# Segmented attention with memory beside a Fourier mixing: the order inside an attention piece, the lead of the row loads, the layout of the stored values

## The chip, the cores and the metric

The kernel runs on one core of one Trainium2 chip, as one launch. The metric is the time on the device in microseconds (us), lower is better. Engines are named as in the profile: PE (matmuls), DVE (VectorE), ACT (ScalarE), POOL (GpSimd), and SP (SyncE), whose queue SPq issues every DMA of this kernel.

## The reference

Two independent parts share the launch, and their outputs stand side by side in the last axis. B is 1, S is 2048, D is 576.

```
# part A: H = 32 heads of Dh = 18, N = 4 segments of L = 512
q, k, v = heads(x @ wq), heads(x @ wk), heads(x @ wv)
for s in range(N):
    logits = qs @ ks^T * Dh**-0.5 + mask   # mask: -1e9 where the key is later than the query
    a_dot  = softmax(logits) @ vs
    pq     = phi(qs)                       # phi(t) = t + 1 for t > 0, else exp(t)
    a_mem  = (pq @ M) / (pq @ z + 1e-6)
    o      = g * a_mem + (1 - g) * a_dot   # g = sigmoid(beta), one per head
    M += phi(ks)^T @ vs ;  z += sum(phi(ks))
A = concat(o) @ wo
# part B
B = dft_seq_re @ (x @ dft_hid_re^T) - dft_seq_im @ (x @ dft_hid_im^T)
out = concat([A, B], axis=-1)
```

## The kernel before, in words

Products in float32 are made from parts: a rounded high part and the remainder, three matmuls for each product. Queries and keys are cut into three bf16 parts, and six pairs of parts (6 x 18 = 108 rows, `NPAIR`) are stacked on the contraction axis, so that one matmul makes scores.

**Projection (first 235 us).** Four segments, one after the other. `project_qk(s, m)` makes nine blocks of queries and keys (m = 0 to 3 queries, 4 to 7 keys, 8 the rest of both); its inner `rest` makes the second and third part and sends them to DRAM (`qd`, `kd`). `project_v(s, j)` makes values for 128 rows and sends them, in three parts with a column of ones, to `vd`: 55 columns a head, 220 for a group of four heads. `load_wv` loads the weights of the values; each is split three ticks later by `split_wk`.

**Attention (235 to about 990 us).** Heads are taken in 32 groups G of four (eight groups in each segment). A loop over pieces p handles two heads in each: `attention()` yields eight times in a piece, after slots 0 to 7, whose weights are `SLOTS`. After each yield the driver runs `tick()`, which calls everything that `later(n, ...)` put off to this tick, and then as much of `dense()` (part B) as the weight stands for. So the order on every engine is fixed when the program is built: the order of the calls is the order of each engine's queue, and no engine overtakes in its own queue. What belongs to heads 2p and 2p + 1 is spread over later pieces by `F_LAG` = 2, `T_LAG` = 3 and `V_LAG` = 4.

- The first head of a piece ("even"): `s_fill` makes scores and DVE takes their row maxima; `t_fill` makes the scores again, transposed, three pieces later; ACT takes the exponential, and `pv` multiplies with the values four pieces after `s_fill`. `t_fill` reads 111 rows of `qs`: the 108 and three more that hold the row maxima.
- The second head ("odd"): `f_fill` makes scores and maxima, `f_exp` the exponential, `f_split_hi` and `f_split_lo` two fp16 parts `hl` (ACT, DVE, POOL), and `f_turn` turns them with a DMA transpose on SP into `ptt`, which `pv` reads.
- `stack_load(G)` loads twelve blocks of 72 KB, six to `qs` and six to `ks`, four in each of the next three ticks, and after `lag` ticks the values `vst`. There are three buffers of `qs` and `ks` (`G % 3`). `s_fill` of group G starts with slot 0 of piece 2G; the last reader of the same buffer is `t_fill` kind 2 of group G - 3, in slot 4 of piece 2G - 2.
- `maxima(p // 2)` runs in slot 4 of every odd piece, when both even heads of the group have their maxima. `maxima_transpose` turns them on PE a few ticks later, copies them on ACT to `mt`, sends them to DRAM (`md`) with a DMA in the next tick, and some ticks later a second DMA brings them as three rows into `qs` (`qs<-md`). The first `t_fill` of group G, in slot 1 of piece 2G + 3, needs these three rows.

PSUM has three banks for part B (`d`), two for scores (`s`), two for transposed scores (`t`), one for `pv`.

**Output (last 65 us).** Part A's heads are joined, transposed and multiplied by `wo`.

Of the kernel before, what the change touches and what calls it, by code (L numbers as in the profile page):

```python
# [15 lines left out]
BF16 = mybir.dt.bfloat16  # L16
AF = mybir.ActivationFunctionType
# [5 lines left out]
S, D, H, DH, NSEG, L = 2048, 576, 32, 18, 4, 512  # L23
P = 128
# [5 lines left out]
NPAIR = 108  # L30
# [6 lines left out]
def infini_attention_and_fnet(ctx: ExitStack, tc: tile.TileContext, xT, wqk, w8, wv, wo, beta, xtT, cT, hT, out):  # L37
    nc = tc.nc
    act, dve, pool, pe = nc.scalar, nc.vector, nc.gpsimd, nc.tensor
    dma = nc.sync.dma_start  # L40
    ctx.enter_context(tc.manual_schedule())
    const = ctx.enter_context(tc.tile_pool(name="const", bufs=1))
    dram = ctx.enter_context(tc.tile_pool(name="dram", bufs=1, space=DRAM))
# [1 line left out]

    qd = [dram.tile([D, 3, L], BF16, name=f"qd{s}") for s in range(NSEG)]
    kd = [dram.tile([D, 3, L], BF16, name=f"kd{s}") for s in range(NSEG)]
    vd = [dram.tile([P, 4, 8, 220], BF16, name=f"vd{s}") for s in range(NSEG)]
    amd = [dram.tile([P, D], F32, name=f"amd{t}") for t in range(NT)]
    md = [dram.tile([24, P], BF16, name=f"md{g}") for g in range(32)]  # L50
    yd = [dram.tile([P, D], F32, name=f"yd{t}") for t in range(NT)]
# [2 lines left out]
    def split(hi, lo, raw, lo_engine=None):  # L54
        act.activation(hi, raw, AF.Copy)  # L55
        (lo_engine or dve).tensor_tensor(lo, raw, hi.bitcast(F32), OP.subtract)  # L56
# [10 lines left out]
    g = const.tile([P, H], F32, name="g")  # L67
# [8 lines left out]
    def chain(o, terms):  # L76
        for n, (a, b) in enumerate(terms):
            pe.matmul(o, a, b, start=n == 0, stop=n == len(terms) - 1)  # L78
# [3 lines left out]
    def later(n, fn, *a):  # L82
        due.setdefault(clock[0] + n, []).append((fn, a))
# [84 lines left out]
        later(3, split_wk, WV, k, load_w(wv, D, k))  # L168

    for k in range(5):  # L170
        later(3 + k, load_wv, k)
    later(5, gates)

    pq_hi = sb.tile([P, 5, L], F32R, name="pq_hi")
# [6 lines left out]
    for i in range(2):  # L181
# [5 lines left out]
        t = sb.tile([P, H, 55], BF16, name=f"vs{i}")  # L187
# [13 lines left out]
    def qk_terms(s, m):  # L201
        xh, xl, xt = X[s]
        W, c = (WQ, m) if m < 4 else (WK, m - 4) if m < 8 else (W8, 0)
        cs = slice(c * P, (c + 1) * P)
        terms = []
        for k in range(4):
            terms += [(W[0][k][:, cs], xh[k]), (W[0][k][:, cs], xl[k]), (W[1][k][:, cs], xh[k])]
        return terms + [(W[2][:, cs], xt), (W[3][:, cs], xt)]
# [20 lines left out]
    def project_qk(s, m):  # L229
        if m in FIRST:  # L230
            o = FIRST.pop(m)
        else:
            o = ps.tile([P, L], F32, name="qk", tag="acc", bufs=4)
            chain(o, qk_terms(s, m))
        if m >= 4 and s < 3:
            KF[m] = sk.tile([P, L], F32, name="kf", bufs=5)
            act.activation(KF[m], o, AF.Copy)
        p = sb.tile([P, 3, L], BF16, name="p", bufs=4)
        r = sb.tile([P, L], F32, name="r", bufs=2)
        act.activation(p[:, 0], o, AF.Copy)  # L240
        dve.tensor_tensor(r, o, p[:, 0], OP.subtract)  # L241
        if s and (m < 4 or m == 8):
            n = P if m < 4 else 64
            c = m if m < 4 else 4
            phi(sb, "q", o[:n], n, pq_hi[:n, c], pq_lo[:n, c])

        def rest():
            act.activation(p[:, 1], r, AF.Copy)
            pool.tensor_tensor(p[:, 2], r, p[:, 1], OP.subtract)
            if m < 8:  # L250
                later(1, dma, (qd if m < 4 else kd)[s][(m % 4) * P:(m % 4 + 1) * P], p)
            else:
                later(1, dma, qd[s][4 * P:], p[:64])
                later(1, dma, kd[s][4 * P:], p[64:])

        later(1, rest)
# [9 lines left out]
    def project_v(s, j, meanwhile):  # L266
        xh, xl, xt = X[s]
        js = slice(j * P, (j + 1) * P)
        vs = vs_bufs[j % 2]
        r = sb.tile([P, H, DH], F32, name="vr", bufs=2)  # L270
        for h in range(2):
            cs, hs = slice(h * 288, (h + 1) * 288), slice(16 * h, 16 * h + 16)
            o = ps.tile([P, 288], F32, name="v", tag="acc", bufs=4)
            terms = []
            for k in range(4):
                terms += [(xh[k][:, js], WV[1][k][:, cs]), (xh[k][:, js], WV[0][k][:, cs]),
                          (xl[k][:, js], WV[0][k][:, cs])]
            terms += [(xt[:, js], WV[2][:, cs]), (xt[:, js], WV[3][:, cs])]
            chain(o, terms)
            o = o.rearrange("p (h d) -> p h d", d=DH)  # L280
            act.activation(vs[:, hs, 18:36], o, AF.Copy)
            if s < 3:
                split(vn[j % 2][0][:, hs, :DH], vn[j % 2][1][:, hs, :DH], o)
            dve.tensor_tensor(r[:, hs], o, vs[:, hs, 18:36], OP.subtract)
            next(meanwhile, None)
        if s < 3 and j == 3:
            for k in range(2, 5):
                split_x(s + 1, k)

        act.activation(vs[:, :, 36:54], r, AF.Copy)  # L290
        pool.tensor_tensor(vs[:, :, 0:18], r, vs[:, :, 36:54], OP.subtract)
        later(1, dma, vd[s][:, j], vs.rearrange("p (g h) c -> p g (h c)", g=8))

    started = set()

# [88 lines left out]
    qs_bufs, ks_bufs, VS = [], [], {}  # L384
# [18 lines left out]

    NG = 32

    def stack_load(G, lag=23):
        if G >= NG:
            return
        s, g8 = divmod(G, 8)
        rows = slice(g8 * 72, g8 * 72 + 72)  # L410
        for buf, src, parts in ((qs_bufs[G % 3], qd[s], QPARTS), (ks_bufs[G % 3], kd[s], KPARTS)):
            for c, part in enumerate(parts):
                later(1 + c // 2, dma, buf[18 * c:18 * c + 18],
                      src[rows, part, :].rearrange("(h d) t -> d h t", d=DH))

        def values():
            VS[G] = sa.tile([P, 4, 220], BF16, name="vst", bufs=3)
            dma(VS[G], vd[s][:, :, g8])
        later(lag, values)

    for s in range(NSEG):
# [277 lines left out]
    def maxima(G):  # L699
        m, b = NEGM[G % 2], MB[G % 2][:, :24].rearrange("p (c n) -> p c n", c=3)  # L700
        r = sa.tile([P, 8], F32, name="negx", bufs=2)
        pool.tensor_copy(b[:, 0], m)
        pool.tensor_tensor(r, m, b[:, 0], OP.subtract)
        pool.tensor_copy(b[:, 1], r)
        pool.tensor_tensor(b[:, 2], r, b[:, 1], OP.subtract)
        later(5, maxima_transpose, G)

    def maxima_transpose(G):
        t = ps.tile([P, P], BF16, name="trm", tag="t")
        pe.transpose(t, MB[G % 2], ident16)  # L710
        w = sa.tile([24, P], BF16, name="mt", bufs=2)
        act.activation(w, t[:24], AF.Copy)
        later(1, dma, md[G], w)
        later(5, dma, qs_bufs[G % 3][NPAIR:NPAIR + 3, 0:4:2], md[G].rearrange("(c h n) t -> c h (n t)", c=3, h=2))

    def t_fill(n, kind):
        G, h = divmod(n, 4)
# [71 lines left out]
    F_LAG, T_LAG, V_LAG = 2, 3, 4  # L789
# [3 lines left out]
    def attention():  # L793
        for p in range(NP + V_LAG):
            def even(lag, fn, *a):
                if 0 <= p - lag < NP:
                    fn(2 * (p - lag), *a)

            def odd(lag, fn, *a):
                if 0 <= p - lag < NP:  # L800
                    fn(2 * (p - lag) + 1, *a)

            if p == 2:
                stacks(sa, 2)
            if p == NP + 1:
                o_load(0)
                o_load(1)
            if p % 2:
                stack_load(p // 2 + 1)
            even(0, s_fill, 0)  # L810
            odd(F_LAG + 1, f_exp, 2)
            odd(F_LAG + 1, f_split_hi)
            yield SLOTS[0]
            even(T_LAG, t_fill, 0)
            odd(F_LAG + 1, f_split_lo)
            yield SLOTS[1]
            even(0, s_fill, 1)
            even(T_LAG, t_fill, 1)
            yield SLOTS[2]
            even(0, s_fill, 2)  # L820
            even(V_LAG, pv)
            even(T_LAG, t_lo, 1)
            yield SLOTS[3]
            odd(F_LAG, f_fill, 0)
            even(T_LAG, t_fill, 2)
            if p % 2 and p < NP:
                maxima(p // 2)
            yield SLOTS[4]
            odd(F_LAG, f_fill, 1)
            odd(V_LAG, pv)  # L830
            even(T_LAG, t_hi)
            even(T_LAG, t_lo, 2)
            yield SLOTS[5]
            odd(F_LAG, f_exp, 0)
            if p >= V_LAG:
                pv_out(p - V_LAG)
            yield SLOTS[6]
            odd(F_LAG, f_exp, 1)
            odd(F_LAG, f_fill, 2)
            even(T_LAG, t_lo, 0)  # L840
            odd(F_LAG + 1, f_turn)
            yield SLOTS[7]
# [7 lines left out]
    for w in attention():  # L850
        tick()
        ta += w
        while td / total_d < ta / total_a:
            t = next(d, BREAK)
# [65 lines left out]
```

## Time and profile before

| what | value |
|---|---|
| time, median of 3 runs | 1069.86 us (1066.59 to 1076.57) |
| the profiled execution: its own time, its span | 1068.58 us, 1066.9 us |
| mean granted clock of PE | 0.99 |
| busy share of the span: PE, DVE, ACT, POOL | 97%, 72%, 65%, 57% |
| PE busy from 242 us to 1000 us | 733.0 of 758.0 us |
| DMA queue q1: packets, bytes, share of the 16 DMA engines | 287616, 192.81 MB, 74.5% |
| row loads `qs<-qd` and `ks<-kd` | 384 DMAs of 72 KB |
| `vd<-vs`, `vst<-vd` | 16 DMAs of 440 KB, 32 of 220 KB |
| DMA transposes `ptt<-hl` | 64 |

A group of instructions is told by line, engine, operation and tile, with its busy time, the mean duration of one, and the idle time of its engine just before it with what ended that idle time. Matmuls are pipelined, so their durations overlap; what one costs is the distance from its start to the next one's. "PEclk" is the granted share of PE's clock. SPq's rows are issues: their duration is how long the issue held SP's queue, not how long the data took.

### The profile page before, as it was taken

Reading aid. Unit: us, or ns where it says so; the run is one execution under the profiler, and the core shown is the slowest. Engines: PE = TensorE matmul, PEld = TensorE weight load, DVE = VectorE, ACT = ScalarE, POOL = GpSimd, SP = SyncE. Lnnn points to the kernel's source line nnn. Section 1 sums busy time; section 2 is a strip of 40 time slices with the busy share of each in tenths; the row PEclk is TensorE's granted clock in tenths of the full one; section 3 lists DMA queues with packets and bytes.
Section 4 is the critical chain, followed back from the end, with each engine's and each line's share of the span. In section 5 each row is a group of like instructions: output and inputs, shape, how many; then the busy total and the mean of one; then the engine's idle time right before and its main releaser. Section 6 shows DMA issues by size and latency. Waiting matters only on the chain.

```text
span 1066.9 us, 25805 instructions
## 1 busy us (share of the span) xinstructions
PE 1031.3 (97%) x9464; PEld 952.7 (89%) x9464; DVE 764.1 (72%) x2095; ACT 695.3 (65%) x1474; POOL 602.8 (57%) x655
## 2 busy tenths in 40 slices
PE   9999999999999999999999999999899998999998
PEld 8888989889998999888988899999898898889998
DVE  6545647574887787678888888889778788776343
ACT  6667575654876777676776777776666676666233
POOL 2456565755765667556666676666565566557000
PEclk9999999999999999999999999999999999999999
DMA  7525253366668888798988999799898999878474
GB/s 237 179 81 182 85 182 136 123 232 181 148 158 196 195 181 198 172 200 216 203 194 191 206 187 177 167 207 198 206 207 187 219 206 192 218 175 182 139 203 142
DMA packets 287742, 194.45 MB, mean 182 GB/s; under 512 B 210496, under 2 KB 242816, under 8 KB 287616
## 3 DMA queue, kind: packets, MB, share of 16 engines
q1 hardware_dynamic: 287616, 192.81, 74.5%
q8 instruction: 74, 1.21, 0.5%
q14 instruction: 52, 0.43, 0.1%
HBM read 106.84 MB, written 43.97 MB: 141 GB/s over the span
## 4 chain that ended last, share of the span: by engine, by line
PE 78%; ACT 7%; DVE 6%; DMA 4%; issue 3%; POOL 2%; SPq 0%; DVEq 0%; POOLq 0%; ACTq 0%
PE d L480 33%; PE s L651 6%; PE d L78 6%; PE v L78 4%; PE d L526 3%; PE pv L768 3%; PE d L527 3%; PE d L528 3%; PE qk L225 2%; DMA craw<-cT 2%; PE pv L769 2%; PE qk L78 1%; DVE r L241 1%; PE look L329 1%; PE t L727 1%
## 5 line engine op out<-in xcount | busy, mean ns | idle before, releaser
L657 DVE CUSTOM_DVE_ANT_0 s<-s,causal 128x512 f32<-128x512 f32 (+3 forms) x512 | 252.9, 496 | 76.3 <-PE s L651 68.5
L56 POOL TENSOR_TENSOR clo<-craw,chi 128x512 fp32r<-128x512 f32 x158 | 217.9, 1380 | 153.6 <-ACT chi L55 122.1
L480 PE MATMUL d<-wide,chi 128*128 128x288 f32 x1408 | 266.1, 306 | 0.0
L480 PEld LDWEIGHTS d<-wide,chi 128*128 128x128 f32 x1408 | 212.2, 191 | 4.6 <-issue 3.7
L480 PE MATMUL d<-wide,clo 128*128 128x288 f32 x704 | 175.9, 317 | 0.0
L680 ACT ACTIVATE pf<-s,nb 128x512 f32<-128x512 f32 (+3 forms) x256 | 127.6, 528 | 57.6 <-DVE nb L672 56.9
L651 PE MATMUL s<-ks,qs 108*128 108x512 bf16 (+3 forms) x512 | 136.1, 307 | 23.8 <-DMA craw<-cT 6.5
L737 ACT ACTIVATE phi<-t 128x384 f16<-128x384 f32 x128 | 62.5, 488 | 102.9 <-PE t L734 83.7
L751 DVE TENSOR_TENSOR plo<-pf,phi 128x384 f16<-128x384 f32 (+1 forms) x128 | 125.6, 981 | 2.3 <-ACT pf L738 2.3
L480 PE MATMUL d<-ab,chi 128*128 128x288 f32 x640 | 126.2, 307 | 0.0
L480 PEld LDWEIGHTS d<-wide,clo 128*128 128x128 f32 x704 | 117.4, 192 | 1.5
L692 POOL TENSOR_TENSOR hl<-pf,hl 128x768 f16<-128x768 f32 x64 | 108.5, 1696 | 0.0
L55 ACT ACTIVATE chi<-craw 128x512 fp32r<-128x512 f32 x160 | 100.6, 629 | 11.6 <-PE d L480 11.5
L738 ACT ACTIVATE pf<-t 128x384 f32<-128x384 f32 (+1 forms) x192 | 99.5, 518 | 11.1 <-PE t L727 10.9
L741 POOL TENSOR_SCALAR_AFFINE_SELECT pf<-pf 128x512 f32<-128x512 f32 x64 | 44.9, 701 | 102.0 <-ACT pf L738 97.4
L480 PEld LDWEIGHTS d<-ab,chi 128*128 128x128 f32 x640 | 99.0, 192 | 0.8
L687 ACT ACTIVATE hl<-pf 128x768 f16<-128x768 f32 (+1 forms) x128 | 87.4, 729 | 2.0
L480 PE MATMUL d<-ab,clo 128*128 128x288 f32 x320 | 84.7, 314 | 0.0
L526 PE MATMUL d<-wide,chi 128*128 128x288 f32 x256 | 82.9, 324 | 0.0
L651 PEld LDWEIGHTS <-qs 108*128 108x128 bf16 x512 | 40.0, 98 | 46.1 <-issue 13.7
L527 PE MATMUL d<-wide,chi 128*128 128x288 f32 x256 | 75.6, 295 | 0.0
L528 PE MATMUL d<-wide,clo 128*128 128x288 f32 x256 | 75.5, 295 | 0.0
(197 smaller groups left out, 2543.0 us busy)
## 6 DMA issues: line engine op xcount, KB each, us to landing
craw<-cT SPq DMA_DIRECT2D x128, 256.0 KB
qs<-qd SPq DMA_DIRECT2D x192, 72.0 KB
ks<-kd SPq DMA_DIRECT2D x192, 72.0 KB
craw<-xtT SPq DMA_DIRECT2D x32, 320.0 KB
out<-y SPq DMA_DIRECT2D x31, 288.0 KB
vd<-vs SPq DMA_DIRECT2D x16, 440.0 KB
vst<-vd SPq DMA_DIRECT2D x32, 220.0 KB
qd<-p SPq DMA_DIRECT2D x16, 384.0 KB
```

The lines of the kernel that those rows point to most:

```text
L55: act.activation(hi, raw, AF.Copy)
L56: (lo_engine or dve).tensor_tensor(lo, raw, hi.bitcast(F32), OP.subtract)
L78: pe.matmul(o, a, b, start=n == 0, stop=n == len(terms) - 1)
L480: pe.matmul(o[h], a, b[:, h * 288:h * 288 + 288], start=start, stop=stop)
L526: pe.matmul(o, xh[:, k], wl[k][:, cs], start=k == 0, stop=False)
L527: pe.matmul(o, xh[:, k], wh[k][:, cs], start=False, stop=False)
L528: pe.matmul(o, xl[:, k], wh[k][:, cs], start=False, stop=False)
L651: pe.matmul(o[:, c:c + w], q[:, i * P:w], k[:, :w], start=True, stop=True)
L657: dve.tensor_tensor_reduce(o[:, c:c + w], o[:, c:c + w], CAUSAL[0][:, L - w:], scale=scale, scalar=-LOWEST, op0=OP.add, op1=OP.min, accum_ ...
L680: act.activation(f[:, FIRST_COL[i]:FIRST_COL[i] + w], o[:, c:c + w], AF.Exp, bias=nb[:, i:i + 1], scale=-1.0)
L692: engine.tensor_tensor(hl[:, 1, a:b], f[:, a:b], hl[:, 0, a:b], OP.subtract)
L751: (pool if kind == 2 else dve).tensor_tensor(lo[:, a:b], f[:, a:b], hi[:, a:b], OP.subtract)
```

## The change

- The driver of the attention: `pv` of the even head stands ahead of `s_fill` kind 2 in slot 3, and `pv` of the odd head ahead of `f_fill` kind 1 in slot 5.
- `stack_load(G)` is called in slot 5 of piece 2G - 2 where it was called in slot 0 of piece 2G - 1: three slots sooner. Its `lag` grows from 23 to 26, so that the values are loaded in the same tick as before.
- `maxima_transpose` comes 4 ticks after `maxima` where it was 5, and `qs<-md` 8 ticks after that where it was 5: one tick sooner for the first step, three later for the second, so two ticks later in all (after slot 7 of piece 2G + 2 where it was after slot 5).
- `vd` is laid out by group: a row of `vd` that belongs to one group is 4 x 220 numbers in one run. The write of one `vs` falls into eight runs of 440 B for each partition, and the load of one `vst` into one run of 1760 B.
- In `rest`, the second part of the key blocks m = 5, 6, 7 is copied by POOL where ACT did it.
- `load_wv` runs two ticks sooner.

```diff
-    vd = [dram.tile([P, 4, 8, 220], BF16, name=f"vd{s}") for s in range(NSEG)]
+    vd = [dram.tile([P, 8, 4, 220], BF16, name=f"vd{s}") for s in range(NSEG)]
...
     for k in range(5):
-        later(3 + k, load_wv, k)
+        later(1 + k, load_wv, k)
...
         def rest():
-            act.activation(p[:, 1], r, AF.Copy)
+            if m in (5, 6, 7):
+                pool.tensor_copy(p[:, 1], r)
+            else:
+                act.activation(p[:, 1], r, AF.Copy)
             pool.tensor_tensor(p[:, 2], r, p[:, 1], OP.subtract)
...
-        later(1, dma, vd[s][:, j], vs.rearrange("p (g h) c -> p g (h c)", g=8))
+        later(1, dma, vd[s][:, :, j], vs.rearrange("p (g h) c -> p g (h c)", g=8))
...
-    def stack_load(G, lag=23):
+    def stack_load(G, lag=26):
...
-            dma(VS[G], vd[s][:, :, g8])
+            dma(VS[G], vd[s][:, g8])
...
         pool.tensor_tensor(b[:, 2], r, b[:, 1], OP.subtract)
-        later(5, maxima_transpose, G)
+        later(4, maxima_transpose, G)
...
         later(1, dma, md[G], w)
-        later(5, dma, qs_bufs[G % 3][NPAIR:NPAIR + 3, 0:4:2], md[G].rearrange("(c h n) t -> c h (n t)", c=3, h=2))
+        later(8, dma, qs_bufs[G % 3][NPAIR:NPAIR + 3, 0:4:2], md[G].rearrange("(c h n) t -> c h (n t)", c=3, h=2))
...
-            if p % 2:
-                stack_load(p // 2 + 1)
             even(0, s_fill, 0)
...
             yield SLOTS[2]
+            even(V_LAG, pv)
             even(0, s_fill, 2)
-            even(V_LAG, pv)
             even(T_LAG, t_lo, 1)
             yield SLOTS[3]
...
             yield SLOTS[4]
+            if p % 2 == 0:
+                stack_load(p // 2 + 1)
+            odd(V_LAG, pv)
             odd(F_LAG, f_fill, 1)
-            odd(V_LAG, pv)
             even(T_LAG, t_hi)
             even(T_LAG, t_lo, 2)
             yield SLOTS[5]
```

## The prediction

> **What bounds the kernel now.** I read the page first (span, busy time, chain), then PE's waits, then PE's and SPq's timelines around the start of a group, then PE's clock there.
>
> ```profile
> span 1066.9 us, 25805 instructions
> PE 1031.3 (97%) x9464; PEld 952.7 (89%) x9464; DVE 764.1 (72%) x2095; ACT 695.3 (65%) x1474; POOL 602.8 (57%) x655
> PE 78%; ACT 7%; DVE 6%; DMA 4%; issue 3%; POOL 2%; SPq 0%; DVEq 0%; POOLq 0%; ACTq 0%
> ```
>
> PE sets the end: 97% busy, 78% of the chain. Anything off PE counts only where PE waits for it. So the question is where PE stands still. In PE's timeline, matmuls with 288 columns start every 0.134 us; I took each start-to-start distance less the usual one for its kind. What is left over is 38 us in 40 places. The largest kind stands at the start of a group, in front of `s_fill` kind 0 (L651) of an even piece. PE's timeline at the start of group 9, then PE's clock in two neighbouring stretches (duration, PE busy, ..., PEclk, DMA share, GB/s):
>
> ```profile
> 430.33 0.43 PE L480 MATMUL d<-wide,clo 128*128 128x288 f32 x2
> 432.88 0.38 PE L651 MATMUL s<-ks,qs 108*128 108x512 bf16 x1 [2.12 <-ACT hl L687]
> ```
> ```profile
> 430.19:433.60 3.41, 1.29 (x10) 0.97 (x9) 1.24 (x5) 2.08 (x4) 0.06 (x1) 1.00 1.27 153
> 433.60:437.01 3.41, 3.41 (x18) 3.26 (x17) 1.00 (x3) 1.25 (x3) 1.59 (x2) 0.50 1.03 260
> ```
>
> PE stands for 2.3 us, and then runs 3.41 us at half clock. The releaser named (ACT) is not the real one: it had long been done. SPq's timeline before it shows what is late (second number: how long the issue holds SP):
>
> ```profile
> 415.51 0.75 SPq L88 DMA_DIRECT2D qs<-md  x1
> 416.43 3.13 SPq L697 DMA_TRANSPOSE ptt<-hl  x1
> ...
> 420.77 0.79 SPq L88 DMA_DIRECT2D qs<-qd  x2
> 421.60 0.77 SPq L88 DMA_DIRECT2D ks<-kd  x2
> 422.42 0.90 SPq L88 DMA_DIRECT2D qs<-qd  x2
> 423.36 0.70 SPq L88 DMA_DIRECT2D ks<-kd  x2
> ...
> 425.43 0.78 SPq L88 DMA_DIRECT2D qs<-qd  x2
> 426.32 1.15 SPq L88 DMA_DIRECT2D ks<-kd  x2
> ...
> 429.23 4.86 SPq L697 DMA_TRANSPOSE ptt<-hl  x1
> ```
>
> The twelve row loads of group 9 are issued from 420.77 to 427.47; their last packet (1024 bytes each, in the trace's packet records) ends at 431.85, and PE goes on 1.03 us later. In 15 of the 32 groups PE waits at this place and the last row packet ended 0.6 to 1.8 us before: 19.7 us in all. Seven of these waits were 2.0 us or longer, and five of the seven were followed by 3.41 us at clock 0.50.
>
> Two rows of PE's timeline matter for what follows, the last reader of the buffer that the next loads fill (`t_fill` kind 2), and the first reader of the three maxima rows (`t_fill` kind 0 of group 7):
>
> ```profile
> 415.26 0.27 PE L734 MATMUL t<-qs,ks 111*128 111x256 bf16 x1
> ...
> 421.44 0.40 PE L727 MATMUL t<-qs,ks 111*128 111x128 bf16 x4
> ```
>
> **Part 1, row loads sooner: a gain.** The first eight loads now follow `t_fill` kind 2 of piece 2G - 2 (415.5 here) instead of standing at the start of the next piece (420.8). The last four come behind the transpose of that piece. By the times below they land some 13 us after `t_fill` kind 2, and `s_fill` comes 16 us or more after it. All 15 waits go: -19.7 us. With them go five stretches at half clock. There, 288-column matmuls start every 0.24 us instead of 0.134, so one stretch loses 3.41 x (1 - 0.134/0.24) = 1.5 us: -7.5 us.
>
> **Part 2, the maxima rows: a loss, and the largest term.** Today `qs<-md` is issued ahead of the transpose of its piece (415.51, transpose 416.43) and PE reads the rows at 421.44: 5.9 us to spare. In the changed build SP's order in an even piece is: eight row loads (the first waits for `t_fill` kind 2 on PE), the transpose, then `qs<-md`, then four row loads. SP overtakes nothing, so the copy waits behind nine issues, the first of them tied to PE. From the end of `t_fill` kind 2:
> - eight row loads: pairs above hold SP 0.70 to 0.90 us; eight took 2.9 to 4.1 us in most groups, 3.0 us with nothing between. I take 3.0.
> - the transpose: 64 of them hold SP 3.0 to 6.0 us; median 3.5 in even pieces, 4.4 in odd pieces, where it stands behind row loads as it now will. I take 3.9. Its data (`hl`, POOL and DVE) are ready before it, mostly before `t_fill` kind 2 ends.
> - `qs<-md`: 0.1 us of gap, 1.85 us from issue to its last packet (median of 32; 1.65 at least), and 1.05 us from last packet to PE (0.95 to 1.2 in the shortest row waits).
>
> Sum 9.9 us. From the end of `t_fill` kind 2 to the start of `t_fill` kind 0 in the next piece there are now 5.3 to 8.2 us, mean 6.1 (415.53 to 421.44 here), and this is dense PE work that the change leaves alone. So PE waits 9.9 - 6.1 = 3.8 us, in front of everything behind it. Groups 1 to 29 have row loads in front (the last two groups load no more): 29 x 3.8 = +110 us. Ends: 2.7 us (2.9 + 3.0 + 2.9 - 6.1) and 5.3 us (3.5 + 4.9 + 3.0 - 6.1), +78 and +154.
>
> **Part 3, clock behind these waits.** Five of seven waits from 2.0 us on were followed by 3.41 us at 0.50; the other two, like the longest at 816.49 (2.45 us), lay across a border of the 3.41 us stretches that the clock's rows step in, with less than 1.9 us on either side. A wait of 3.8 us always has 1.9 us on one side. I take a slow stretch for each, and 1.3 of its 1.5 us, since part falls into the wait: 29 x 1.3 = +38 us (0 to +44).
> The Trainium skill ("TensorE: Matmul & The Clock Gate", "What's actually happening") says that the clock halves after an idle window of about 3.4 us. By that rule the five slow stretches would not be there, and few of the new ones: with 4 us for part 3 and no gain of 7.5 us the sum would be 1159 us. The trace speaks against it: 2.0 us of idle time were enough at 931.66.
>
> **Part 4, the rest.**
> - `load_wv` two ticks sooner: PE waits at 38.02 and 38.81 for the last split of `wv` (1.3 and 0.66 us). -2 us, 0 at worst.
> - `pv` first: same matmuls, other order. In before, `s_fill` kind 2 waited three times for a score bank (0.4, 1.2, 1.0 us); `pv` now covers such waits. It also hands DVE its scores 20 x 0.026 = 0.5 us later. DVE has room: it waited 68.5 us for L651. -1.5 us, ends -2.6 and, were every one of 64 pieces to pay 0.5, +33.
> - POOL copies twelve key parts (L248, ACT, 0.624 us each). The trace has no such copy on POOL; its bounds are 0.25 us (the 8-column copy, L702) and 1.19 us (the two-input subtraction, L249). Near the second: 1.0 us. Copy and subtraction make 2.2 us for a block, under the 14 x 0.227 = 3.2 us that PE spends on it; that work hides it. Without cover, three segments wait up to 3 us each for `kn` (L199): 0 to +9.
> - `vd` by group: a write has 1024 packets of 440 B instead of 128 of 3520 B. At the 34 ns of today's 440 B packets that is 2.2 us over 16 DMA engines instead of 1.2, sixteen times, in a stretch whose DMA share is 0.47, with a whole attention phase before most are read. The loads shrink from 512 packets to 128, off PE's path. 0.
>
> Sum against the profiled execution's own time: 1068.6 + 110 + 38 - 19.7 - 7.5 - 2 - 1.5 = **1186 us** (1.7 us of it lie outside the span; that execution is 1.3 us under the median).
>
> **Rivals.**
> - *The copy of the maxima is in time, the row loads decide* (faster). Place: `t_fill` kind 0; it decides if the chain above takes 6.1 us or less. Then only the gains stay: 1068.6 - 19.7 - 7.5 - 3.5 = 1038 us. For it: 15 real waits. Against it: the shortest transpose alone holds SP for 3.0 us and the copy takes 2.6 us at least, so the eight loads would have 0.5 us. 6%.
> - *Gain and loss cancel*: waits of about 1 us, without loss of clock: 29 x 1 - 31 leaves 1067 us. It needs transposes and loads at their shortest and PE's stretch at its longest (8.2 us). 3%.
> - *The waits come, the clock stays*: 1186 - 38 = 1148 us. For it: two of seven kept the clock. 13%.
> - *SP falls further behind*: transposes of 4.9 us as at 429.23, part B's loads (`craw`) among the row loads; waits of 5.3 us, each with its slow stretch: 1068.6 + 154 + 44 - 31 = 1236 us. For it: the new wait of SP for PE holds all later issues, `craw` too. Against: the wait on PE gives SP time to catch up. 10%.
>
> **How the numbers follow.** The forecast has 68%; its own range is 1150 to 1225. The range 1125 to 1230 takes in the third rival and half of the fourth. Over 1% is about what a measurement of this kernel can tell from no change: faster 6%, within it 3%, slower 91%.
>
> **What would show it.** PE's waits should have a new first row: L727, some 29 times, about 4 us each; PE's clock should be at 0.50 in some 29 stretches, mean near 0.96. In SPq's timeline `qs<-md` should follow a transpose by less than 0.2 us, and the first row load should start as `t_fill` kind 2 ends. The waits of L651 at group starts should be gone. Wrong would be: no wait at L727, or row loads that do not wait for PE; a time under 1060 us.

## The result and the profile after

The changed kernel takes 1202.01 us (median of 4 runs, 1198.59 to 1208.85) against 1068.71 us for the kernel before on the same chip: 1.124 times as long, with a 95% interval from 1.1163 to 1.1317. The profiled execution took 1203.26 us, 134.7 us more than that of before.

The page after (span, busy time, shares of the chain that ended last), its granted clock, and the first rows of PE's waits (engine, line, what it waited for: us in total, times, longest us):

```profile
span 1201.5 us, 25714 instructions
PE 1074.8 (89%) x9464; PEld 993.4 (83%) x9464; DVE 751.8 (63%) x2095; ACT 691.9 (58%) x1462; POOL 607.7 (51%) x667
PE 64%; DMA 8%; SPq 7%; DVE 6%; POOL 5%; ACT 4%; issue 2%; POOLq 0%; ACTq 0%; DVEq 0%
```
```profile
core 0: 1201.5 us, clock 0.939
```
```profile
PE t L730 <- DMA qs<-md: 104.6, 30, 5.8
PE s L654 <- ACT pf L683: 5.3, 11, 1.1
```

PE issues the same 9464 matmuls. Its busy time grew by 43.5 us; the other 91 us of the span's growth are idle time, and one row of waits alone has 104.6 us: `t_fill` kind 0 (L730, L727 before) waits for the maxima rows. SPq and DMA, together 4% of the chain before, now hold 15%. The first row of SP's own waits is new, too: its queue is held for PE's last reader of the buffer (`t_fill` kind 2, L737). The second fence is a row of SP's waits in before that is gone in the changed kernel; it matters below.

```profile
SPq L88 <- PE t L737: 95.6, 24, 6.4
```
```profile
SPq L88 <- DMA md<-mt: 39.8, 26, 3.2
```

One such place, SPq's timeline (start, us that the issue held SP's queue), then PE's:

```profile
499.24 0.67 SPq L88 DMA_DIRECT2D qs<-qd  x2
...
501.44 0.70 SPq L88 DMA_DIRECT2D ks<-kd  x2
502.24 0.36 SPq L371 DMA_DIRECT2D craw<-cT  x1
502.71 3.96 SPq L700 DMA_TRANSPOSE ptt<-hl  x1
506.72 0.73 SPq L88 DMA_DIRECT2D qs<-md  x1
```
```profile
498.94 0.27 PE L737 MATMUL t<-qs,ks 111*128 111x256 bf16 x1
504.72 0.42 PE L483 MATMUL d<-wide,clo 128*128 128x288 f32 x2
508.85 0.59 PE L730 MATMUL t<-qs,ks 111*128 111x128 bf16 x4 [3.71 <-DMA qs<-md]
```

The first row load is issued as L737 ends (499.21), eight loads and one of part B later the transpose starts, the copy of the maxima follows 0.05 us after the transpose has let the queue go, and PE goes on 9.6 us after L737. PE has dense work for 5.9 us of that. Three neighbouring stretches of the clock around this wait (duration, PE busy, ..., PEclk, DMA share, GB/s):

```profile
503.90:507.30 3.40, 1.24 (x9) 1.09 (x8) 1.97 (x5) 1.84 (x3) 0.00 (x0) 0.99 1.16 239
507.30:510.70 3.40, 1.85 (x10) 1.84 (x10) 0.00 (x0) 1.11 (x2) 0.49 (x1) 0.50 0.50 124
510.70:514.10 3.40, 3.40 (x18) 2.94 (x17) 0.98 (x4) 0.87 (x2) 3.00 (x3) 0.50 0.73 241
```

The wait runs from 505.14 to 508.85, 2.2 us of it in the first stretch. The second is at half clock, holds the other 1.5 us of idle time, and is followed by a third at half clock with PE fully busy.

### The profile page after: what moved, and what is told of

Read it like the earlier page. It is cut to its first block, busy times and chain, and to the rows that moved or that the text cites. A ratio compares the mean times of both kernels' runs of the same rounds, so it can differ in the third digit from the quotient of the medians.

```text
span 1201.5 us, 25714 instructions
## 1 busy us (share of the span) xinstructions
PE 1074.8 (89%) x9464; PEld 993.4 (83%) x9464; DVE 751.8 (63%) x2095; ACT 691.9 (58%) x1462; POOL 607.7 (51%) x667
## 4 chain that ended last, share of the span: by engine, by line
PE 64%; DMA 8%; SPq 7%; DVE 6%; POOL 5%; ACT 4%; issue 2%; POOLq 0%; ACTq 0%; DVEq 0%
PE d L483 26%; SPq L700 6%; DMA qs<-md 6%; PE s L654 5%; PE d L78 5%; PE pv L771 3%; PE v L78 3%; PE qk L78 3%; POOL clo L56 3%; PE d L529 2%; PE d L530 2%; PE d L531 2%; PE t L730 2%; DVE s L660 2%; PE pv L772 2%
## 5 line engine op out<-in xcount | busy, mean ns | idle before, releaser
L56 POOL TENSOR_TENSOR clo<-craw,chi 128x512 fp32r<-128x512 f32 x158 | 212.3, 1344 | 190.8 <-ACT chi L55 169.1
L483 PE MATMUL d<-wide,chi 128*128 128x288 f32 x1408 | 283.6, 321 | 0.0
L483 PEld LDWEIGHTS d<-wide,chi 128*128 128x128 f32 x1408 | 228.3, 204 | 5.1 <-issue 3.2
L483 PE MATMUL d<-wide,clo 128*128 128x288 f32 x704 | 187.2, 334 | 0.0
L483 PE MATMUL d<-ab,chi 128*128 128x288 f32 x640 | 131.8, 317 | 0.0
L483 PEld LDWEIGHTS d<-wide,clo 128*128 128x128 f32 x704 | 127.4, 206 | 1.8 <-issue 0.2
L730 PE MATMUL t<-qs,ks 111*128 111x128 bf16 x256 | 28.9, 245 | 104.6 <-DMA qs<-md 104.6
L754 DVE TENSOR_TENSOR plo<-pf,phi 128x384 f16<-128x384 f32 (+1 forms) x128 | 116.2, 908 | 2.4 <-ACT pf L741 2.4
L730 PEld LDWEIGHTS <-ks 111*128 111x128 bf16 x256 | 19.2, 106 | 111.8 <-issue 107.0
L483 PEld LDWEIGHTS d<-ab,chi 128*128 128x128 f32 x640 | 104.2, 201 | 1.7 <-issue 0.9
L529 PE MATMUL d<-wide,chi 128*128 128x288 f32 x256 | 84.4, 330 | 0.0
L530 PE MATMUL d<-wide,chi 128*128 128x288 f32 x256 | 76.5, 299 | 0.0
```

The lines of the kernel that those rows point to most:

```text
L483: pe.matmul(o[h], a, b[:, h * 288:h * 288 + 288], start=start, stop=stop)
L529: pe.matmul(o, xh[:, k], wl[k][:, cs], start=k == 0, stop=False)
L530: pe.matmul(o, xh[:, k], wh[k][:, cs], start=False, stop=False)
L754: (pool if kind == 2 else dve).tensor_tensor(lo[:, a:b], f[:, a:b], hi[:, a:b], OP.subtract)
```

## Experiments

Three go from the changed kernel (1, 2 and 4), to find what of it costs the time; nine go from before, to find what its parts are worth alone. Ratios are to the kernel before on the same chip.

**1. The delays of the maxima rows put back in the changed kernel.** All other parts stay.

```diff
-        later(4, maxima_transpose, G)
+        later(5, maxima_transpose, G)
-        later(8, dma, qs_bufs[G % 3]...
+        later(5, dma, qs_bufs[G % 3]...
```

> The changed kernel, only the two delays of the maxima rows put back to 5 and 5, so that the copy into qs stands ahead of the row loads and the transpose again. Theory (the copy waits behind eight row loads and a transpose): the 29 waits at t_fill kind 0 and the slow clock behind them go, the gain of the sooner row loads stays, 1035 to 1050 us. Rival (the row loads at their new place, which make SP wait for PE, or the new order of pv cost the time): still 1150 us or more. Rival (the sooner row loads bring nothing because PE then waits elsewhere): about 1069 us.

Measured: 1065.48 us, 0.9958 (0.9932 to 0.9984). The waits of L730 for the rows are gone and with them the whole loss: the late copy is its cause. But the gain of the sooner row loads, some 30 us by the prediction, isn't there. PE's waits for DMA in this kernel have a new first row:

```profile
PE pv L771 <- DMA ptt<-hl: 7.9, 11, 3.0
```

The transposes now stand behind row loads and come late for `pv` (none of these waits in before), and `t_fill` kind 1 waits 4.1 us for ACT's copy of the maxima (L733; 1.2 us in before). The waits at group starts did shrink, from 20.6 us to 3.8 us. The attention also starts 3.9 us later (experiment 9), and SP's waits for the landing of `md<-mt` are still 33.3 us in 24 places (experiments 3 and 5).

**2. The read one tick sooner.** The copy then stands behind four row loads and ahead of the transpose, not behind eight and the transpose.

```diff
-        later(8, dma, qs_bufs[G % 3]...
+        later(7, dma, qs_bufs[G % 3]...
```

> The changed kernel with the copy of the maxima rows one tick sooner (7 where it was 8): it then stands behind four of the row loads and ahead of the transpose. Theory: from t_fill kind 2 to PE 1.5 + 0.1 + 1.85 + 0.5 = 4 us, less than the 6.1 us there are; no wait, 1035 to 1050 us. Rival (it is the row loads ahead of the copy that matter, not the transpose): about half of the loss stays, 1120 us or more.

Measured: 1057.93 us, 0.9891 (0.9835 to 0.9947). L730 waits 0.8 us in two places where it waited 104.6 us. One tick takes back 144 us. The tick moves the copy ahead of four row loads and of the transpose at once, and no run separates these two; by the times measured in the changed kernel (below), eight loads without the transpose would bring the rows to PE after some 5.7 us, inside the 6.1 us that PE has, so the transpose is needed for the loss (an estimate). The time is 8 us above the upper end of what I expected, since `pv` waits 6.4 us for `ptt` and the start is 4 us later (below).

**3. The late maxima alone, on the kernel before.**

```diff
-        later(5, maxima_transpose, G)
+        later(4, maxima_transpose, G)
-        later(5, dma, qs_bufs[G % 3]...
+        later(8, dma, qs_bufs[G % 3]...
```

> The kernel before, only the delays of the maxima rows changed to 4 and 8: the copy stands behind the transpose, but no row load that waits for PE stands ahead of that transpose. Theory (both are needed: the row loads tie the transpose to t_fill kind 2): from the profile before, end of the transpose + 0.05 + 1.84 + 0.45 us comes up to 2.7 us after t_fill kind 0 is due in 20 of 31 groups, 28 us in all at most, less if the transpose starts sooner: 1075 to 1100 us. Rival (the transpose alone makes the loss): 1170 us or more.

Measured: 1059.86 us, 0.9914 (0.9888 to 0.994): faster than before, a miss. Without row loads tied to PE in front, the copy is late only sometimes:

```profile
PE t L727 <- DMA qs<-md: 11.9, 12, 2.5
```

and something else improved by more than these 12 us (the forecast was 1075 us or more). SP's waits for the landing of `md<-mt` (39.8 us in 26 places in before, the fence above) don't occur at all. In before the read of `md` stands so close behind its write that SP's queue stands still for about 1.5 us a group until the write has landed; what is behind it, transposes and row loads, waits with it. Experiment 5 shows how much sooner the row loads come when most of this is gone.

**4. Idle work in the wait.** Forty matmuls of 128 columns, their result overwritten at once, stand ahead of each late `t_fill` kind 0 of the changed kernel. They wait for nothing late and keep PE busy.

```diff
         o = ps.tile([P, L], F32, name="t")
+            for _ in range(40 if h == 0 and 1 <= G <= 29 else 0):
+                pe.matmul(o[:, :P], ident16, ident16, start=True, stop=True)
```

> The changed kernel with 40 idle matmuls of 128 columns (2.2 us at full clock) on PE ahead of t_fill kind 0 of groups 1 to 29; they are overwritten by the product that follows. They stand where PE waits for the maxima rows, so they lengthen nothing, but PE idles 1.5 us there and not 3.7. Theory (part of the loss is PE's clock, halved after each wait): the clock stays at 1.00 and the time falls by 40 to 55 us, to 1148 to 1165 us, though work was added. Rival (the waits alone are the loss): 1200 us or a little more.

Measured: 1154.92 us, 1.0782 (1.0714 to 1.085), 47 us less than the changed kernel with 1160 matmuls more. The profiled execution of it:

```profile
core 0: 1143.6 us, clock 0.996
```
```profile
PE t L732 <- DMA qs<-md: 34.0, 28, 2.7
```

The rows still come as late (what is left of each wait is 1.2 us); only the half-clock stretches went. They cost 47 us by the medians. The profiled span is 57.9 us shorter than that of the changed kernel, 2.0 us of it ahead of the attention; the other executions of this kernel had mean clocks of 0.987 to 0.990, so some of the stretches stayed in them.

**5. The best delays alone, on the kernel before** (4 and 7).

```diff
-        later(5, maxima_transpose, G)
+        later(4, maxima_transpose, G)
-        later(5, dma, qs_bufs[G % 3]...
+        later(7, dma, qs_bufs[G % 3]...
```

> The kernel before, only the delays of the maxima rows changed to 4 and 7: the copy into qs has two ticks more after the write to DRAM, and still stands ahead of the transpose of its piece. Theory (in the kernel before SP stands still for the landing of the write, and transpose and row loads behind it come late): the wait of SP for md goes, the row loads start one to two microseconds sooner, the waits at group starts go as in the run with 4 and 8, and no wait comes at t_fill kind 0: 1045 to 1053 us. Rival (those waits went because the copy stood behind the transpose): 1062 us or more.

Measured: 1050.18 us, 0.9843 (0.9818 to 0.9869): the fastest of all, 1.6% under before. SP's wait for the landing, and the first row of PE's waits:

```profile
SPq L88 <- DMA md<-mt: 11.6, 12, 2.4
```
```profile
PE s L651 <- ACT pf L680: 5.8, 8, 1.2
```

Start-to-start, PE's waits at group starts fell from 20.6 us in 15 places to 8.4 us in 7. The last row packet of a group now ends 2.67 us before the rows are due (median of groups 4 to 31), 1.17 us in before, with the row loads called at the same place in the program. The mean clock rose from 0.990 to 0.997: one stretch at half clock in the attention where before has five. The shorter waits (12.2 us) and these four stretches at 1.5 us each make up the gain.

**6. The sooner row loads on top of 5** (`stack_load` in slot 5, `lag` 26).

> The kernel before with two of the changes: the row loads three slots sooner, and the maxima rows with delays 4 and 7. Order of pv, start of the kernel and layout of the values as before. Theory (with the write of md no longer waited for, sooner row loads bring nothing more and only push the transpose back, for which pv then waits): 1 to 6 us more than the run with 4 and 7 alone, 1047 to 1058 us. Rival (sooner row loads are a gain of their own): less than that run by 5 us or more.

Measured: 1053.27 us, 0.9865 (0.9841 to 0.9888). Given the better delays, the sooner loads bring nothing: 3 us more than without them, in overlapping intervals. The rows of PE's waits that replace those at the group starts:

```profile
PE pv L768 <- DMA ptt<-hl: 2.6, 4, 0.9
PE t L727 <- DMA qs<-md: 2.3, 3, 1.2
```

**7. `pv` first, alone.**

> The kernel before, only pv ahead of s_fill kind 2 and of f_fill kind 1. Theory (the order of pv is worth little by itself; the waits of pv for ptt come from row loads ahead of the transpose): within 3 us of before, no more than 2 us of waits for ptt. Rival (pv first waits for the transpose by itself): 6 to 12 us more, with waits of pv for ptt.

Measured: 1071.48 us, 1.0036 (1.0013 to 1.006). A small loss, about 4 us, a little more than the 3 us I allowed; the waits at group starts are 23.7 us (20.6 before), and the attention has six half-clock stretches where before has five. Which part of the order costs it I didn't separate.

**8. The parts at the start, together:** `load_wv` sooner, POOL's copies, `vd` by group.

> The kernel before, only the three edits that touch the projection: weights of the values two ticks sooner, POOL's copies of key parts, values by group in DRAM. Theory (they lengthen the projection, as the profile of the changed kernel says: attention starts 4 us later): 1071 to 1075 us where before has about 1069. Rival (the prediction's: 2 us are won): 1066 to 1068 us.

Measured: 1066.66 us, 0.9992 (0.9975 to 1.0008), no change, where a loss was expected. In the profiled execution the first write of the values is 1.9 us sooner than in before (42.88 against 44.80 us), but the attention starts 2.6 us later (238.1 against 235.5 us); it is shorter afterwards. At the end of the projection ACT waits for the write of the values to let `vs` go (first line; the second is the same wait in before). This wait comes with POOL's copies and not with the layout, as experiments 9 and 10 show:

```profile
ACT vs L284 <- DMA vd<-vs: 6.5, 1, 6.5
```
```profile
ACT vs L281 <- DMA vd<-vs: 0.2, 1, 0.2
```

**9. `vd` by group, alone** (the layout, its write and its load).

> The kernel before, only vd laid out by group. Theory (its writes of 440 B pieces land later, their last packet 3 to 6 us after the issue instead of 2 to 3.5, and ACT, which refills vs, waits for one of them in the last segment): ACT waits 6 us or more for vd<-vs before attention starts, PE waits 4 us there instead of 2, attention starts 1 to 3 us later than 235.5 us. Rival (the prediction's: the write is hidden): start within 0.5 us of 235.5. Whole time within 4 us of before in either case.

Measured: 1068.92 us, 1.0027 (1.0003 to 1.0052). The attention starts at 241.4 us, 5.9 us later than in before. Of this, 1.7 us is there ahead of the first write of the values (46.53 against 44.80 us), with a half-clock step at 39.01 that before has not, so the layout can't have caused it; 4.2 us come behind that write. ACT's wait for a write was 2.2 us here, not the 6 I expected, so the end of the projection isn't the reason. The trace shows another, the load of the next rows of x (`raw`), which SP issues right behind a write of the values. First SP, ACT and PE here, then ACT in before:

```profile
58.11 0.53 SPq L88 DMA_DIRECT2D vd<-vs  x1
58.73 0.62 SPq L103 DMA_DIRECT2D raw<-xT  x1
65.58 0.63 ACT L112 ACTIVATE xt<-raw 128x512 fp32r<-128x512 f32 x1 [4.27 <-DMA raw<-xT]
69.54 0.73 PE L304 MATMUL m<-vnh,knh 128*128 128x152 f32 x3 [2.03 <-DVE knh L198]
```
```profile
60.23 0.63 ACT L112 ACTIVATE xt<-raw 128x512 fp32r<-128x512 f32 x1 [0.62 <-DMA raw<-xT]
```

The last packet of that load ends 6.5 us after its issue, 3.7 us in before. ACT waits for it, POOL (`vs`) for ACT, DVE (`knh`) for POOL, and PE for DVE; PE's wait is followed by two half-clock steps. All seven traces with this layout have it (ACT 4.0 to 5.2 us, PE 1.8 to 3.0 us); the seven without it have at most 0.6 us on ACT and no wait of PE there. So the layout costs time through a load that shares the queue with its writes. Whether the 1024 packets ahead of it hold up the load at the issue or in the DMA engines, no run separates.

The attention is some 6 us shorter (729.2 against 734.9 us, to the last scores of 512 columns); it has two half-clock stretches where before has five, which is most of that.

**10. POOL copies, alone** (a single execution).

> The kernel before, only the copies of key parts on POOL. If POOL's copies hold up the start: attention begins 1 us or more after 235.5 us, with waits of PE for kn. If they are hidden as the prediction says: within 0.5 us of 235.5. A copy should take 0.7 us, as in the changed kernel.

Measured: 1066.97 us, attention from 235.8 us (235.5 before). The copy takes 753 ns on POOL. ACT's long wait of experiment 8 is here, with the layout of before:

```profile
ACT vs L284 <- DMA vd<-vs: 6.6, 1, 6.6
```

PE's last wait of the projection is 4.0 us (2.0 in before), but two waits of 0.75 us are gone; in sum the start stays.

**11. `load_wv` two ticks sooner, alone** (a single execution).

> The kernel before, only the weights of the values loaded two ticks sooner. Prediction: the waits of 1.3 and 0.7 us near 38 us go and attention starts 2 us sooner, at 233.5 us. Rival (the loads crowd out the next segment's rows of x, for which ACT waits 5 us near 57 us, and DVE and PE after it): the 2 us come back as a wait of PE near 65 us, start at 235.5 us or later.

Measured: 1060.89 us, attention from 232.2 us, 3.3 us sooner: the waits near 38 us are gone. The first write of the values is 1.9 us sooner (42.86 us); the rest is the half-clock step of before at 218.56, which this execution has not. For the total, executions of before spread from 1062.93 to 1073.44 us beside this one, so only the start is counted here.

**12. The best delays with `vd` by group.**

> The kernel before with the delays of the maxima rows 4 and 7 and vd by group. Theory (the loads of vst become shorter and clear SP's DMA engines sooner, but PE is not waiting for them any more; the writes cost up to 2 us at the start): within 3 us of the run with 4 and 7 alone, 1048 to 1053 us. Rival (shorter loads make transposes and row loads land sooner, which is worth something): 1043 to 1047 us.

Measured: 1056.52 us, 0.99 (0.9869 to 0.9932), some 6 us more than with the delays alone and above the 1048 to 1053 us I expected. The attention takes the same time (715.2 us, 716.3 with the delays alone); it starts at 242.7 us instead of 235.9. So the layout costs time at the start here too, and the 6 us that it won in the attention of before don't appear.

## Why the prediction held, and where it did not

**The main term, +110 us: right, by its own steps.** PE's waits at L730 make 108.4 us, start to start, in 29 groups: 3.74 us each, against 3.8. The chain from the end of `t_fill` kind 2, means over these groups: the first load starts 0.03 us after it; the eight loads take 3.25 us (3.0 said); the gap is 0.24 us; the transpose holds SP 3.96 us (3.9); the copy's last packet ends 1.84 us after its issue (1.85). From there to PE it is 0.50 us, not 1.05: that term was read from waits for the last of twelve 72 KB loads, and this is one small copy. The loads and the gaps, 0.5 us too short in the sum, cancel it. The steps of the chain were right, but that the sum fits this well (9.88 us against 9.9) is luck. PE's stretch without the wait is 6.14 us (6.1). Experiments 1 and 2 show that the copy's place is the cause: both take the whole loss back, the second by one tick.

**The clock, +38 us: the right mechanism, undersized.** After 27 of the 29 waits the clock was at 0.50 for at least one step of 3.41 us, as the forecast had it. But 13 of the 30 slow stretches of the whole run lasted two steps. The term assumed one for each wait, since it took 1.3 us for each; experiment 4 gives 47/29 = 1.6 us by the medians and 57.9/29 = 2.0 us by the profiled executions. The trace itself gives an estimate between them: 136.5 us of the attention are at half clock, PE is busy in 120 of these, and 120 x (1 - 0.134/0.24) = 53 us, 1.8 us for each wait. In before all the slow stretches of the attention had ended after one step. A wait of 3.7 us can reach into the stretch that is already slow and leave idle time there, 1.5 us in the one from 507.30, and then the next is slow as well. That this idle time renews it is my reading of the doubles; no run varied it by itself. In the attention of this trace it fits all 28 stretches: the first slow step held 0.52 us or more of idle time in the 12 doubles, 0.52 us or less in the 16 singles. It can't be the whole rule: a single at 946.78 in experiment 1 held 0.60 us, and the first of the two slow steps at 69.72 in experiment 9 held none. The Trainium skill ("TensorE: Matmul & The Clock Gate", "What's actually happening") would have let the clock fall only after an idle window of about 3.4 us; the trace disagrees, since a wait of 2.62 us that ended at 753.54 in the changed kernel was enough. The rival without loss of clock (1148 us) falls with the mean clock of 0.939 and with experiment 4.

**The row loads, -19.7 and -7.5 us: the waits went, the reason was half of it.** In the changed kernel the rows land 8.7 us (median) before they are due, and the waits at group starts shrank from 20.6 us in 15 places to 2.8 us in 5. So the term was there in the sum. What the prediction did not see is one reason why rows were late in before. SPq's timeline just ahead of the lines quoted there:

```profile
412.62 0.35 SPq L88 DMA_DIRECT2D md<-mt  x1
...
413.07 0.43 SPq L368 DMA_DIRECT2D craw<-cT  x1
415.51 0.75 SPq L88 DMA_DIRECT2D qs<-md  x1
```

The queue issues nothing from 413.50 to 415.51: the read waits for the write to land, and the transpose and the row loads behind it wait with it. I had read these rows as issues only. Loading three slots sooner is one cure; spreading write and read is the better one (experiment 5: 17 us; experiment 6: nothing on top). Experiment 5 has the write a tick sooner and the read a tick later than before; which of the two does more was not tried.

**The rest.** `load_wv` -2: right (1.9 us at the first write of the values). POOL's copies 0: right in sum (708 ns each in the changed kernel, 1.0 us estimated), though not hidden, since ACT's and PE's waits at the end of the projection grew (experiment 10). `vd` 0: wrong. The projection's writes do not hide: from their first write to the attention it takes 194.9 to 197.4 us in the seven traces with this layout, 189.3 to 191.3 us in the seven without. The attention starts 4.2 us later in the changed kernel, where the prediction had it 2 us sooner. What failed is the cover: I took the DMA share of 0.47 as room, and looked at who reads `vd` but not at what is issued behind its writes, the load of x for which ACT, POOL, DVE and PE then wait in turn. The writes themselves land 2.9 to 4.8 us after their issue (experiment 9), 2.1 to 3.5 us in before, though a 440 B packet took 27 or 28 ns, less than the 34 ns assumed. `pv` first -1.5: wrong sign, +0.36% in experiment 7.

**The sum.** 108.4 of wait, 47 of clock (the medians' value), 4.2 at the start, less 17.8 of row waits and less the 7.5 put down for before's slow stretches, make 134.3 us against 134.7 measured between the profiled executions. So close a fit is luck as well: with the 53 or 57.9 us from the traces in place of 47, some 6 or 11 us of gain would stay unassigned, and that is not settled. The forecast was 17 us low by the profiled executions (1186 against 1203.3); by this sum, 9 of it come from the clock, 6 from the start, 2 from the row waits and 1.5 from `pv`, less 1.6 from the main term.

**The rivals.** Three are settled. "In time" (1038 us) had the wrong price as well as the wrong chance: with the copy in time the same program takes 1057.93 or 1065.48 us, not 1038: `pv`'s waits for the transposes (6.4 or 7.9 us) and the later start (4 us) take part of the gain. "Cancel" needed waits of 1 us; they are 3.7. "SP further behind" had the longest wait right (5.8 us in one place) but not the mean.

## What to carry to other kernels

On a queue that keeps its order, a transfer that is moved later is priced by what stands ahead of it there, and by what that in turn waits for: here one tick, which put a transpose and four more loads ahead of a copy behind loads tied to PE, was worth 144 us. A read-back of a small DRAM buffer close behind its write holds the whole queue until the write has landed; putting ticks between them made unrelated loads come sooner and was worth 17 us, and moving those loads on top of it brought nothing (the loads moved by themselves, with all else as before, were not run). For a moved load, list also the waits of the issuing queue in the profile before, not only the waits of the engine that sets the end. For a write that is cut into smaller runs, look at the loads that are issued behind it.

## What the runs showed of the hardware

- More work made the program faster: 1160 matmuls without use in PE's waits took 47 us off by the medians; the waits stayed, and the mean clock went from 0.930 to 0.939 up to 0.987 to 0.996.
- A half-clock step with 1.5 us of idle time in it was followed by another, in which PE was fully busy; 13 of the 30 slow stretches were doubles (6.83 us). In the attention of the changed kernel the first step of each double held 0.52 us or more of idle time, that of each single 0.52 us or less.
- Waiting for the landing of a 6 KB write cost the issuing queue 39.8 us in 26 places.
- The same 440 KB in runs of 440 B instead of 3520 B landed 2.9 to 4.8 us after the issue instead of 2.1 to 3.5 us, and a load issued right behind such a write ended 6.5 us after its issue instead of 3.7 us.
